# Weights issued sooner, token scores and token values later in the step, memory transposes of 64 columns

## The chip, the cores and the metric

The kernel runs on one core of one Trainium2 chip. The metric is the device time of one execution in microseconds (us). Three runs of the kernel before took 1035.26, 1035.57 and 1038.22 us; the median is 1035.57 us.

The core has five engines with an instruction queue each: TensorE (PE, with its weight loads shown apart as PEld), VectorE (DVE), ScalarE (ACT), GpSimd (POOL) and SyncE (SP). SP issues most DMAs; ACT and POOL can issue some too. An instruction at the head of a queue that has to wait for another engine holds up all that stands behind it on its own engine.

## The reference

A pre-normed attention with a memory that is carried from segment to segment, and a feed-forward layer behind it. The sequence of 2048 tokens (width 640) is cut into 64 segments of 32 tokens. Each segment attends to itself and to 8 memory rows, and the memory rows of its output are the memory of the next segment. So the 64 segments follow one another:

```python
mem = mem0
for s in range(n_seg):                       # 64
    h = concat([mem, xs], axis=1)            # 8 + 32 rows of 640
    q, k, v = h @ Wq, h @ Wk, h @ Wv         # 32 heads of 128
    p = softmax(mask(q @ k.T * scale))
    o = (p @ v) @ Wo
    mem = o[:, :M]                           # the next segment's memory
    outs.append(o[:, M:])
h = x + attention(layernorm(x))
out = h + relu(layernorm(h) @ w1 + b1) ** 2 @ w2 + b2
```

## The kernel before

Four segments are a block `b` of 128 tokens, and a segment is a step `s = 4*b + sp`. A program for each engine is written out by hand: `tc.manual_schedule(engines=None)` (L104) means that each engine runs its instructions in the order in which the Python code issues them. So where a line stands in `step` decides what it waits behind.

A segment's 40 rows are split in two. 32 of them (8 memory rows and the first 24 tokens) go through the step itself: they fill 32 columns of the array, and four such matmuls stand side by side in the 128 columns (`proj`, L194 to L204; the profile writes 128*32). The last 8 tokens of each segment, the tails, are projected for four segments at once, ahead of time: `tail_units` (L257) makes units of four matmuls each, and lists of them (`fill`) are run where PE would otherwise wait. A tail's queries and keys are put in place by `tails_in` (L312, POOL), its values are written to DRAM (`tail_out`, L272) and read back by `tails_v_in` (L321). The output product of four segments' tails is another list of units (`wo_tail_units`, L285).

One step (`step`, L368), in the order of PE's queue:

- four projections, two of queries and two of keys (L204, twenty matmuls each), each evacuated by ACT (L220, L222, L393) and turned over by DVE (L225, L396); POOL spreads the memory's queries (`spread`, L357);
- the memory rows' scores, first half (`scores(0)`, L404 and L409), then DVE's maximum (L415) and ACT's exponential (L418);
- two groups of the value projection (L473), half of the tokens' scores (`token_scores(0)`, L480 and L484), the other three groups (L490);
- DVE divides and turns over the memory's probabilities (`soft2(0)`, L424 to L428);
- two groups of the second value projection, `scores(1)`, `token_scores(1)`;
- `token_values` of the segment before (L343, L348), `values(0)` of this one (L437, L442), the last three groups of values (L512);
- DVE takes the tokens' maximum and subtracts it (L520, L522);
- the output product (`wo_rounds`, L236) in three parts, with `values(1)` after the first and one fill unit after the second (L526 to L532);
- ACT's exponential of the tokens' scores (L535), DVE's sum and reciprocal (L537, L539), POOL's products (L541, L544);
- `wo_out` (L239): ACT copies half of the product (L243), DVE adds the other half (L244); that is the segment's output `o`. Meanwhile PE runs 4 or 6 fill units (L556);
- `mem_to_hT` (L304): twenty small matmuls turn the memory rows of `o` into the columns that the next step's projections need, and DVE copies them into `hT` (L310); then `tails_in`, and the rest of the fill;
- DVE turns over the tokens' probabilities (L562, L568), for the token values of the next step.

The PSUM tiles are few: three for projections (`mm`), one (`chn`) shared by `scores`, `wo_rounds` and `mem_to_hT`, one (`po`) for the values.

Ahead of the loop, the weights are loaded by SP in the order in which they stand in the code: x of block 0, the memory, the tail rows, Wv (five DMAs of 1 MB), the next tail rows, Wq, x of block 1, Wk, and Wo in four DMAs (L134 to L145 and L709 to L717). `start` (L662) projects the first step's 40 rows and the first tails as the weights come in; with its v, `step` is called as "ready" and leaves out its own projections. Behind the loop, the feed-forward layer runs over four tiles of 512 tokens (L787 to L846).

Of the kernel before, what the change touches and what calls it, by code (L numbers as in the profile page):

```python
# [16 lines left out]
def kernel(  # L17
# [16 lines left out]
    nc = tc.nc  # L34
# [43 lines left out]
    ident = const.tile([128, 128], BF16)  # L78
    make_identity(nc, ident[:])
# [22 lines left out]
    oTts = [const.tile([128, H, 32], BF16, name="oTt%d" % k) for k in range(2)]  # L102

# [25 lines left out]
    o_ring = [const.tile([128, DH], BF16, name="o%d" % k) for k in range(5)]  # L129
    for o in o_ring:  # L130
        nc.gpsimd.memset(o[64:128], 0.0)
    o0 = o_ring[-1]
    nc.vector.memset(o0[0:64], 0.0)
    load_x(0)  # L134
    for ch in range(2):
        nc.sync.dma_start(out=o0[32 * ch:32 * ch + M, :].rearrange("m (c f) -> m c f", f=64),
                            in_=A_mem0[0].rearrange("m (c t f) -> t m c f", t=2, f=64)[ch])
    load_tail_rows(0)
    load_w(wv, A_Wv)
    def load_wo():  # L140
        wov = A_Wo.rearrange("h e d -> e h d")
        for n in range(2):
            for j in range(2):
                hs = slice(16 * j + n, 16 * j + n + 15, 2)
                nc.sync.dma_start(out=wo[:, hs, :], in_=wov[:, hs, :])  # L145
# [28 lines left out]
    def ln_transpose(b):  # L174
# [6 lines left out]
        def out():  # L181
            if isinstance(b, tuple):
                hTt = s2.tile([128, DC, 4, TL, 4], BF16, tag="hTt", name="hTt")
                nc.scalar.copy(out=hTt[:].rearrange("p c b k s -> p (c b) s k"),
                               in_=pt[:, 0:640].rearrange("p (a s k) -> p a s k", s=4, k=TL))
                hTts[b[1]] = hTt
                return
# [59 lines left out]
    fill, late, mid, win = [], [], [], []  # L247
# [24 lines left out]
    def tail_out(b, which, n, ps):  # L272
        row = parked.pop(0) if which == "v" and 0 < b and parked else rowtile()[:]
        evac_row(which, row, ps)
        if which == "v":
            eng = nc.sync if b else nc.scalar
            eng.dma_start(out=vt_d[b, 2 * n:2 * n + 2].rearrange("j r f -> r j f"),
                          in_=row.rearrange("r (j f) -> r j f", j=2))
# [25 lines left out]
    def mem_to_hT(o, hT4, sp):  # L304
        pm = chn.tile([128, 512], F32, tag="ch", name="pm")
        for c in range(DC):
            for q in range(4):
                nc.tensor.matmul(pm[32 * q:32 * q + 32, c * M:(c + 1) * M], lhsT=o[:, (2 * c + q % 2) * 32:(2 * c + q % 2 + 1) * 32],  # L308
                                 rhs=ident[:, q // 2 * 32:q // 2 * 32 + M], start=True, stop=True)
        nc.vector.tensor_copy(out=hT4[:, :, sp, 0:M], in_=pm[:, 0:DC * M].rearrange("p (c m) -> p c m", m=M))  # L310

    def tails_in(b, sp):  # L312
        q, k = [tails[b][w][:].rearrange("p h (k s) -> p h s k", s=4)[:, :, sp, :] for w in "qk"]
        nc.gpsimd.tensor_copy(out=qT[:, :, SEG:NK], in_=q)
        nc.gpsimd.tensor_copy(out=kT[:, :, SEG:2 * SEG].rearrange("p h (j k) -> p h j k", k=TL),  # L315
                              in_=k.unsqueeze(2).to_broadcast([128, H, 4, TL]))

    vt4s = {}
# [17 lines left out]
    def token_values(s, v, vt4, po):  # L336
# [3 lines left out]
        for i in range(HG):  # L340
            for g in range(G):
                r = slice(32 * g, 32 * g + 32)
                nc.tensor.matmul(po[:, g, i * 32:(i + 1) * 32], lhsT=v[r, i * E:(i + 1) * E], rhs=pTk[r, i, :],  # L343
                                 start=(i == 0), stop=False, skip_group_check=True)
# [23 lines left out]
    def step(b, sp, v=None):  # L368
# [62 lines left out]
        def values(n, pT, po):  # L431
            c0 = 256 + n * 4 * M
            for j in range(4):
                i = n * 4 + j
                for g in range(G):
                    r = slice(32 * g, 32 * g + 32)
                    nc.tensor.matmul(po[:, g, c0 + j * M:c0 + (j + 1) * M], lhsT=v[r, i * E:(i + 1) * E],  # L437
                                     rhs=pT[r, j * M:(j + 1) * M], start=(s == 0 and i == 0), stop=False,
# [11 lines left out]
        if not last and not ready:  # L450
            spread(0)
        if not last:
# [7 lines left out]

        if ready:
            tails_v_in(0, nc.gpsimd)
# [11 lines left out]
        sk = mmtile()  # L474
        skv = sk[:, 0:HG * NK].rearrange("p (i k) -> p i k", k=NK)

        def token_scores(n):
            if n == 0:
                for g in range(G):
                    nc.tensor.matmul(skv[32 * g:32 * g + 32, :, M:NK], lhsT=ident[:, 0:32], rhs=mask[:],  # L480
                                     start=True, stop=False, skip_group_check=True)
            for j in range(4):
                for g in range(G):
# [395 lines left out]
```

## Time and profile before

| what | value |
|---|---|
| three runs | 1035.26, 1035.57, 1038.22 us |
| profiled execution, its own time | 1037.09 us |
| its span in the profile | 1034.9 us, 2.2 us less than its time |
| PE busy | 973.5 us, 94% of the span, 26960 matmuls |
| DVE busy | 616.4 us, 60% |
| ACT busy | 533.5 us, 52% |
| POOL busy | 311.4 us, 30% |
| loads and stores by DMA | 51.58 MB |
| stretch up to 71.3 us | start and first step |
| stretch from 71.3 to 885.4 us | steps 1 to 62 |
| rest | last step and feed-forward layer |

A line of the timeline reads: start in us from the span's start, duration in us, engine, line, operation, output <- inputs, shape and count, and in brackets how long the engine had been idle ahead of it and what ended the wait. "issue" is time in which an engine waited for nothing that the profile shows. In a matmul's shape, 128*32 is the part of the array that it uses (rows by columns), and 128x512 is its moving operand. DVE, ACT and POOL busy shares are averages; what counts for a step is the chain from one step's `hT` to the next.

### The profile page before, as it was taken

What the parts mean: (1) busy time and instruction counts of PE and PEld (TensorE: products, weight loads), DVE (VectorE), ACT (ScalarE), POOL (GpSimd) and SP (SyncE); (2) the same over time, 40 slices, a digit from 0 to 9 for tenths busy, and PEclk for the clock granted to TensorE, in tenths of its full rate; (3) what the DMA queues carried; (4) which work ended last, traced back from release to release, by engine and by line L of the source; (5) the groups of instructions that cost most, each with busy time, mean ns of one, the idle gap of its engine ahead of it and who ended that gap; (6) DMA issues with size and microseconds to landing.
All of it is one profiled execution on the core that took longest, in us unless ns stands there. A gap on an engine that the chain in (4) does not pass through costs nothing.

```text
span 1034.9 us, 58969 instructions
## 1 busy us (share of the span) xinstructions
PE 973.5 (94%) x26960; PEld 572.4 (55%) x26960; DVE 616.4 (60%) x1740; ACT 533.5 (52%) x1225; POOL 311.4 (30%) x805
## 2 busy tenths in 40 slices
PE   4779899999999999999999999999999999999998
PEld 2335455555655555565555565565556565555565
DVE  2245666766666666666666666666665576565432
ACT  2425555555555555555555555555555555534431
POOL 1033333333333332232323232323233333343210
PEclk9989999999999999999999999999999999999999
DMA  8960100000100000000000000000000110512200
GB/s 321 405 203 26 23 7 28 9 22 8 28 14 22 14 25 23 14 21 14 27 14 21 15 27 14 22 15 27 15 21 9 46 34 6 195 55 71 77 26 26
DMA packets 39112, 51.58 MB, mean 50 GB/s; under 512 B 6160, under 2 KB 34960, under 8 KB 36944
## 3 DMA queue, kind: packets, MB, share of 16 engines
q1 hardware_dynamic: 38000, 47.30, 13.8%
q8 instruction: 210, 3.44, 1.4%
q14 instruction: 38, 0.31, 0.1%
q0 software_dynamic: 320, 0.26, 0.1%
q10 hardware_dynamic: 544, 0.26, 0.1%
HBM read 38.37 MB, written 9.44 MB: 46 GB/s over the span
## 4 chain that ended last, share of the span: by engine, by line
PE 87%; DMA 5%; issue 3%; DVE 2%; ACT 1%; POOL 0%; SPq 0%; DVEq 0%; ACTq 0%; POOLq 0%
PE ps L204 48%; PE pw L236 15%; PE y L830 6%; PE ps L798 5%; PE ps L236 3%; DMA xt<-in_A_x_dram 3%; PE po L437 2%; PE po L343 2%; PE sm L409 2%; DMA wq<-in_B_w_dram 1%; PE ps L484 1%; PE pm L308 1%; PE ps L480 1%; DMA vt<-vt_d 1%; DVE o L244 1%
## 5 line engine op out<-in xcount | busy, mean ns | idle before, releaser
L204 PEld LDWEIGHTS <-hT 128*32 128x32 bf16 x7680 | 193.4, 96 | 178.4 <-issue 14.5
L236 PE MATMUL pw<-wo,oT 128*32 128x320 bf16 x4224 | 184.9, 300 | 5.4 <-issue 4.3
L204 PE MATMUL ps<-wv,hT 128*32 128x512 bf16 x2520 | 171.2, 380 | 3.3 <-issue 2.6
L204 PE MATMUL ps<-wq,hT 128*32 128x512 bf16 x2520 | 158.2, 379 | 4.9 <-DVE hT L310 4.9
L204 PE MATMUL ps<-wk,hT 128*32 128x512 bf16 x2520 | 158.1, 379 | 0.1
L236 PEld LDWEIGHTS <-oT 128*32 128x32 bf16 x4224 | 104.7, 96 | 59.5 <-issue 11.8
L220 ACT ACTIVATE row<-ps 128x512 bf16<-128x512 f32 x156 | 93.3, 599 | 74.1 <-PE ps L204 72.8
L541 POOL TENSOR_TENSOR pkt<-ek,rk 128x64 bf16<-128x64 bf16 x64 | 18.8, 294 | 366.1 <-DVE rk L539 366.1
L225 DVE STREAM_TRANSPOSE qT<-row 128x512 bf16<-128x512 bf16 x128 | 90.2, 705 | 53.0 <-ACT row L220 53.0
L222 ACT CAST row<-ps 128x512 bf16<-128x512 f32 x115 | 67.9, 591 | 38.6 <-PE ps L204 38.5
L315 POOL COPY kT<-kTt 128x1024 bf16<-128x1024 bf16 x64 | 71.7, 1120 | 12.6 <-DVE kTt L225 12.6
L362 POOL COPY qz<-qT 128x96 bf16<-128x96 bf16 x126 | 33.4, 265 | 139.0 <-DVE qT L225 135.3
L204 PEld LDWEIGHTS <-hTt 128*32 128x32 bf16 x1920 | 53.1, 99 | 36.6 <-issue 6.0
L243 ACT COPY otmp<-pw 64x320 f32<-64x320 f32 x66 | 27.9, 422 | 81.0 <-PE pw L236 81.0
L353 ACT CAST oT<-po 128x512 bf16<-128x512 f32 x128 | 68.7, 589 | 1.6
L244 DVE TENSOR_TENSOR o<-pw,otmp 64x320 bf16<-64x320 f32 x66 | 31.8, 482 | 61.0 <-ACT otmp L243 61.0
L513 ACT CAST v<-ps 128x512 bf16<-128x512 f32 x63 | 36.9, 585 | 60.6 <-PE ps L204 60.6
L225 DVE STREAM_TRANSPOSE kT<-row 128x512 bf16<-128x512 bf16 x65 | 46.0, 709 | 29.7 <-ACT row L222 29.7
L537 DVE TENSOR_REDUCE zk<-ek 128x8 f32<-128x320 bf16 x64 | 31.1, 486 | 53.6 <-ACT ek L535 53.6
L830 PE MATMUL y<-wq,wk 128*128 128x320 bf16 x416 | 60.9, 299 | 0.0
L393 ACT CAST row<-ps 128x256 bf16<-128x256 f32 x126 | 40.7, 375 | 30.1 <-PE ps L204 30.1
L491 ACT CAST v<-ps 128x512 bf16<-128x512 f32 x63 | 36.9, 585 | 30.5 <-PE ps L204 30.5
(114 smaller groups left out, 1635.2 us busy)
## 6 DMA issues: line engine op xcount, KB each, us to landing
wv<-in_A_Wv_dram SPq DMA_DIRECT2D x5, 1024.0 KB
wq<-in_A_Wq_dram SPq DMA_DIRECT2D x5, 1024.0 KB
wk<-in_A_Wk_dram SPq DMA_DIRECT2D x5, 1024.0 KB
wo<-in_A_Wo_dram SPq DMA_DIRECT2D x4, 1280.0 KB
vt<-vt_d SPq DMA_DIRECT2D x60, 64.0 KB
xt<-in_A_x_dram SPq DMA_DIRECT2D x20, 160.0 KB
vt_d<-row SPq DMA_DIRECT2D x22, 128.0 KB
wq<-in_B_w_dram SPq DMA_DIRECT2D x1, 2080.0 KB
```

The costliest lines, as they stand in the source:

```text
L204: nc.tensor.matmul(ps[32 * k:32 * k + 32, :], lhsT=lhs(c), rhs=wr[:, c, n, k], start=(c == 0), stop=(c == DC - 1))
L220: nc.scalar.mul(out=row, in_=ps, mul=scale)
L222: nc.scalar.copy(out=row, in_=ps)
L225: nc.vector.transpose(out=dst[:, n * 16:(n + 1) * 16, 0:32], in_=row.rearrange("p (h e) -> p h e", e=32))
L236: nc.tensor.matmul(pw[32 * j:32 * j + 32, 0:DH], lhsT=lhs(p), rhs=wov2[:, head(p), ch], start=(h == 0), stop=(h == 15))
L244: nc.vector.tensor_tensor(out=o[0:64], in0=pw[0:64, 0:DH], in1=tmp[0:64], op=ALU.add)
L315: nc.gpsimd.tensor_copy(out=kT[:, :, SEG:2 * SEG].rearrange("p h (j k) -> p h j k", k=TL), in_=k.unsqueeze(2).to_broadcast([128, H, 4, TL]))
L353: nc.scalar.copy(out=oTg[:, n, :, :, M:NK], in_=po[:, :, n * 128:(n + 1) * 128].rearrange("p g (j q) -> p g j q", q=32))
L393: nc.scalar.copy(out=row[:, u * 256:(u + 1) * 256], in_=ps[:, u * 256:(u + 1) * 256])
L491: nc.scalar.copy(out=v[:, 0:512], in_=ps0[:])
L798: nc.tensor.matmul(ps[:], lhsT=w1[:, c, fc * 128:(fc + 1) * 128], rhs=hnT[:, c, :], start=(c == 0), stop=(c == DC - 1))
L830: nc.tensor.matmul(y[:, hh, 0:DH], lhsT=f1T[:, fc, k * 128:(k + 1) * 128], rhs=w2[:, fc, cs], start=(fc == 0), stop=False, skip_group_chec ...
```

## The change

- Loads: the memory is loaded through ACT's queue, so that SP goes on to the tail rows and Wv without waiting; x of block 1 goes behind Wk and Wo, and its norm and transposes go from `start` into steps 1 and 2; Wo comes in six pieces, the heads that the product needs first ahead of the others; the stores of the tails' values of blocks 1 to 4 are put off to step 1.
- Start: the tails' queries and keys are put in place in halves; `tails_v_in(0)` and ten units of block 4's tail values go between the query and key projections, and ten units of block 1's tail keys behind the key projection, instead of into the first step.
- Step: `token_scores` is one piece and goes behind `values(1)`, between the two halves of the output product; `token_values` goes behind the whole output product, in the place of two of the fill units that stood there; the fill unit within the product is gone. The tokens' exponential goes behind ACT's L243, and the chain behind it goes into the next step in two parts: `soft_a` (L537 to L544) behind the first query projection, `soft_b` (L562 to L568) behind the second. `tails_in` goes ahead of the fill.
- `mem_to_hT`: ten matmuls of 64 columns in place of twenty of 32.

```diff
     def load_wo():
         wov = A_Wo.rearrange("h e d -> e h d")
-        for n in range(2):
-            for j in range(2):
-                hs = slice(16 * j + n, 16 * j + n + 15, 2)
-                nc.sync.dma_start(out=wo[:, hs, :], in_=wov[:, hs, :])
+        for h0, k in ((0, 8), (16, 8), (1, 4), (17, 4), (9, 4), (25, 4)):
+            hs = slice(h0, h0 + 2 * k - 1, 2)
+            nc.sync.dma_start(out=wo[:, hs, :], in_=wov[:, hs, :])
...
     def mem_to_hT(o, hT4, sp):
         pm = chn.tile([128, 512], F32, tag="ch", name="pm")
         for c in range(DC):
-            for q in range(4):
-                nc.tensor.matmul(pm[32 * q:32 * q + 32, c * M:(c + 1) * M], lhsT=o[:, (2 * c + q % 2) * 32:(2 * c + q % 2 + 1) * 32],
-                                 rhs=ident[:, q // 2 * 32:q // 2 * 32 + M], start=True, stop=True)
+            for ch in range(2):
+                nc.tensor.matmul(pm[64 * ch:64 * ch + 64, c * M:(c + 1) * M], lhsT=o[:, c * 64:(c + 1) * 64],
+                                 rhs=ident[:, 32 * ch:32 * ch + M], start=True, stop=True)
...
         project("q", wq, qT, 0)
         if not last and not ready:
             spread(0)
+        run(soft, 1)
...
         elif not ready:
             spread(1)
-
-        if ready:
-            tails_v_in(0, nc.gpsimd)
+        run(soft, 1)
...
-        token_scores(0)
...
-            proj(wv, "half", lhs, 1, ps1, 0, 2)
+            proj(wv, "half", lhs, 1, ps1, 0, 3)
         if not last:
             scores(1)
-        token_scores(1)
-        if not last:
             soft1(1)
...
-        if s:
-            token_values(s - 1, prev["v"], prev["vt4"], po)
         if not last:
             values(0, pT0, po)
             values_out(0, po)
         if not ready:
-            proj(wv, "half", lhs, 1, ps1, 2, DC)
+            proj(wv, "half", lhs, 1, ps1, 3, DC)
...
-        wo_rounds(main, pw, 0, 6)
+        wo_rounds(main, pw, 0, 8)
         if not last:
             values(1, pT1, po)
             values_out(1, po)
-        wo_rounds(main, pw, 6, 8)
-        run(fill, 1)
+        sk = mmtile()
+        skv = sk[:, 0:HG * NK].rearrange("p (i k) -> p i k", k=NK)
+        token_scores(skv)
+        mxk = s1.tile([128, HG], F32, tag="mxk", name="mxk")
+        nc.vector.tensor_reduce(out=mxk[:], in_=skv, op=ALU.max, axis=AX.X)
...
         wo_rounds(main, pw, 8, 16)
...
+        o = wo_out(pw)
         ek = s1.tile([128, HG, NK], BF16, tag="ek", name="ek")
-        nc.scalar.activation(out=ek[:], in_=tk[:], func=ACT.Exp, scale=1.0)
...
+        nc.scalar.activation(out=ek[:], in_=tk, func=ACT.Exp, scale=1.0)
         if s:
+            token_values(s - 1, prev["v"], prev["vt4"], po, last)
             token_out(s - 1, po)
...
-            run(fill, 4 if outs else 6)
+            run(fill, 2 if outs else 4)
             mem_to_hT(o, hT4s[(s + 1) // 4], (s + 1) % 4)
...
+        def soft_a():
+            zk = s1.tile([128, HG], F32, tag="zk", name="zk")
+            nc.vector.tensor_reduce(out=zk[:], in_=ek[:], op=ALU.add, axis=AX.X)
...
+            soft.append(lambda: soft_b(pkt, pk))
+
+        def soft_b(pkt, pk):
+            pTt = s1.tile([128, 2, 32], BF16, tag="pTt", name="pTt")
+            nc.vector.transpose(out=pTt[:], in_=pkt[:].rearrange("p (u j) k -> p u (j k)", u=2))
...
+            pTk = s1.tile([128, HG, 32], BF16, tag="pTk", name="pTk")
+            nc.vector.transpose(out=pTk[:], in_=pk[:])
+            back.append((pTk, pTx))
+
+        soft.append(soft_a)
...
         stream("q", wq, qT)
         for n in range(2):
             spread(n)
-        ln_transpose(1)()
-        units += tail_units(4, "v") + tail_units(1, "q")
+        tails_v_in(0, nc.gpsimd)
+        units += tail_units(4, "v")
+        run(units, 2 * DC)
+        units += tail_units(1, "q")
         stream("k", wk, kT)
+        units += tail_units(1, "k")
+        run(units, 2 * DC)
         run(late, 100)
...
-    load_x(1)
     load_w(wk, A_Wk)
     load_wo()
+    load_x(1)
```

## The prediction, made before the changed kernel ran

> **What bounds the kernel now.** I read the page, then the windows, then the timelines of the start and of one step. Page: the second slice line is PE's, then the queue that brings instructions, then the chain that ended last by engine.
>
> ```profile
> PE   4779899999999999999999999999999999999998
> ...
> q8 instruction: 210, 3.44, 1.4%
> ...
> PE 87%; DMA 5%; issue 3%; DVE 2%; ACT 1%; POOL 0%; SPq 0%; DVEq 0%; ACTq 0%; POOLq 0%
> ```
>
> PE sets the pace but for the first 70 us, so a step lasts as long as PE's work in it plus PE's waits. In the start the loads set it: in the windows (columns: PE, PEld, DVE, ACT, POOL, granted clock, DMA share, GB/s) the DMA engines are full until 60 us and PE's clock falls.
>
> ```profile
> 40.00:60.00 20.00, 14.06 (x272) 6.71 (x268) 5.80 (x13) 6.00 (x13) 4.00 (x6) 0.77 1.05 375
> 60.00:80.00 20.00, 16.20 (x443) 8.69 (x444) 10.09 (x31) 6.87 (x17) 4.29 (x12) 0.91 0.40 116
> ```
>
> The start's timeline: x of block 1 lands only at 35.46 and PE's key projection stands behind it (38.47); then PE waits 5.53 us for the tails' keys; step 1 begins at 71.28.
>
> ```profile
> 35.46 0.89 DVE L152 BATCH_NORM_STATS2 lnst<-xt 128x6 f32<-128x320 bf16 x2 [12.23 <-DMA xt<-in_A_x_dram]
> ...
> 54.62 0.40 PE L409 MATMUL sm<-kT,qz 128*32 128x64 bf16 x16 [5.53 <-POOL kT L315]
> ...
> 71.28 1.26 PE L204 MATMUL ps<-wq,hT 128*32 128x512 bf16 x20 [0.34 <-DVE hT L310]
> ```
>
> The step from 398.20 (first query projection) to 411.91 is the model for the loop:
>
> ```profile
> 402.30 0.71 DVE L225 STREAM_TRANSPOSE qT<-row 128x512 bf16<-128x512 bf16 x1 [0.38 <-ACT row L220]
> ...
> 402.94 0.22 DVE L415 TENSOR_REDUCE mx<-sm 128x1 f32<-128x64 f32 x1
> ...
> 404.28 0.25 DVE L428 STREAM_TRANSPOSE pTm<-pmem 128x64 bf16<-128x64 bf16 x1
> ...
> 405.04 0.29 PE L437 MATMUL po<-pTm,v 32*128 32x8 bf16 x15
> ...
> 406.31 0.09 PEld L437 LDWEIGHTS <-v 32*128 32x128 bf16 x1 [1.07 <-issue]
> ...
> 411.14 0.28 PE L308 MATMUL pm<-ident,o 128*32 128x8 bf16 x20
> ```
>
> DVE runs the last query transpose, then the maximum of `scores(0)`, and its probabilities are ready at 404.53; PE takes them at 405.04. So this chain has 0.45 us to spare, no more. The 1.07 us of "issue" is the other finding: PE stops with all its operands ready. The instruction queue's 210 packets of 16 KB are 257 instructions each for PE's 53920, and four such stops (379, 392, 405, 419 us) lie 768 PE instructions apart, three packets. After such a stop PE goes on 2.5 to 3.6 us after it passed the border one packet back, 3.05 taken as the middle. The Trainium skill ("Runtime: NRT & Kernel Launch", Instruction fetch mechanics) says that blocks of 256 instructions are fetched while the last one runs, mostly hidden; by the rule the stops would be nothing, and here they are not.
>
> Counted from one `scores(0)` to the next, 35 steps with ten fill units last 13.04 us on average (shortest 12.56), 14 steps with a whole output-tail product 13.45, six with five units 12.97, five with none 13.0. In the 49 full ones 0.3 to 0.4 us is such stops.
>
> **The step, part by part** (us from the start of the first query projection; hops of 0.05 between engines as the timeline has them).
>
> Work that PE keeps is conserved: projections 4 x 1.08, `scores` 2 x 0.14, values' projections 2 x 1.08, `values` 0.26 + 0.23, token scores 0.34, token values 0.28, product 64 matmuls 2.16, ten units 2.16, memory transposes 0.13: 12.3. What changes are the waits.
>
> `soft_b` puts L562 and L568 on DVE between the last query transpose and the maximum of `scores(0)`. These two take 0.48 (398.50 to 398.98 in the timeline). POOL's products for them come behind the reciprocal: DVE is free at 2.6, sum 0.5, reciprocal 0.2, POOL 0.3 + 0.6: ready at 4.3, ahead of DVE's 4.74, so no wait there. The maximum goes from 4.74 to 5.22, and everything behind it on DVE with it: L396 to 6.17 and the probabilities from 6.33 to 6.81, ready for PE at 6.86. PE's cover between `scores(0)` and `values(0)` was 0.43 + 0.21 + 0.65 + 0.43 + 0.14 + 0.23 + 0.28; the token scores (0.21 + 0.23) and values (0.28) leave, one group of values (0.22) comes: PE arrives at 4.32 + 0.14 + 1.08 + 0.65 + 0.14 = 6.33. So PE waits 0.53 in front of `values(0)`. Queued behind it are the values' projection and the product; ACT and DVE, waiting for them, are late next.
>
> Token scores stand between `values(1)` and the second half of the product, which needs ACT's L213: 0.61 from the last `values(1)` matmul in the timeline, against 0.11 + 0.34 of cover: 0.15 wait. The first half of the product must wait for DVE's L211: 0 to 0.1, take 0.05. Behind the product, `o` needs 1.30 (409.84 to 411.14), which six units (1.29) hid exactly; four units and token values are 0.86 + 0.28 = 1.14: wait 0.15. Token values also bring a second change of the array's tiling, which fits into this wait. Sum of waits 0.9, from 0.65 (all small ones gone) to 1.1. In their favour, today's wait of 0.12 for ACT's v in front of `values(1)` goes.
>
> Memory transposes: twenty matmuls take 0.13, 6.5 ns each, four side by side, so 26 ns for one place. Ten with two side by side: 0.13 again. But they are in another tiling than their neighbours: where the product is followed by 128-column transposes (L179) it takes 1.19 instead of 1.09. One such change hides in the wait for `o`, the other costs 0.1 (from -0.07, if ten take half of twenty's time, to 0.2). The Trainium skill ("TensorEngine Tiling (Array Packing)", Key Properties) says that a change of tiling mode drains the array, which speaks against this edit; it gives no price. Its cover for DVE's `hT` is now 1.29 of fill instead of 0.65, and 0.65 was enough.
>
> Stops for instructions: a step has 780 instead of 800. Densest run of 256 today: 24 matmuls of projection, `scores(1)`, token scores, values: 2.5 us; in the new order `values(1)`, token scores, half product, token values: 2.1 to 2.3, but the run around `values(0)` is stretched by its wait to 2.9. Sliding the border over the step with 3.05 us per 256, I get 0.55 today (the trace: 0.4) and 0.2 then.
>
> Full step: 12.3 + 0.9 + 0.1 + 0.2 = 13.5 against 13.04: +0.44, bounds -0.1 to +0.8. 49 of them: **+21.6** (-5 to +39). Steps without fill or with five units gain, since token values now cover 0.28 of their 1.3 wait and the rest of units come after: 12.75 against 12.97 and 12.6 against 13.0: 6 x 0.2 + 5 x 0.4 = **-3**.
>
> **The start.** SP now issues Wv at about 1.75 instead of 4.76 (the memory's 1.62 and the wait ahead of it leave; ACT issues them with nothing waiting there until 6.5). The packets run without a hole from 6.3 to 46 (Wk) and 61 us (Wo, 0.36 MB/us), so all comes 3.0 sooner, and x of block 1 (0.16 MB) another 0.4: Wk's last packet at 42.8, Wo's at 57.4. A load is usable some 1.6 behind its last packet (Wk: 46.2, used at 48.03). The keys are then done at 45.3 instead of 49.1, and DVE's seven remaining transposes put the first maximum at 51.1 instead of 55.07; block 0's values are there, where PE waited for them until 62.85. But now the product waits for Wo's last piece, 59.0, where before it began at 66.67 with Wo there: product 0.55, `o` 1.30, `hT` 0.63: step 1 at 61.5. After such idling the clock is at half for about 3.4 us (as 52.4 to 59.3 now), of which I charge 1.3: 62.8, **-8.5** (-11 to -5, the latter if the issue of Wk waits for ACT's stores and leaves a hole). Block 1's transposes go into step 2: **+0.4**. x of block 1 lands at 59.5, ahead of need. Last step: the moved chain hides behind `end_output`'s 64 matmuls: 0, at worst +1.
>
> **Sum.** 1037.1 (profiled) + 21.6 - 3 - 8.5 + 0.4 = 1047.6; the median lies 1.5 under the profiled execution: **1046**. Own range 1038 to 1058.
>
> **Rivals.**
> - *The loop loses less than the start gains.* The point is (8.5 + 3 - 0.4) / 49 = 0.23 us a step. For it: 0.4 us of stops might all be absorbed by the new waits, and the small waits may vanish: 12.3 + 0.65 = 12.95, -0.1 each, 1037.1 - 5 - 11.1 - 1.5 = 1019.5; the middle between that and break-even is 1027. Against it: the 0.48 on DVE and the 0.72 of cover taken from PE are read off the queue's order. Chance 0.20.
> - *Break even:* loss of 0.17 to 0.3 a step, 1035. Chance 0.07.
> - *The start doesn't gain:* Wk waits for a hole in the loads and the clock stays low; the loop loses as forecast: 1054. Chance 0.10, slower too.
> - *Forecast:* 0.63.
>
> So slower 0.73, within 0.3% (3 us, about what these runs can tell from nothing) 0.07, faster 0.20. Range 1024 to 1058: a tenth is left out on either side.
>
> **What would show it.** PE idle of about half a us in front of L437 of `values(0)`, ended by DVE's transpose, in nearly every step; the two transposes of `soft_b` directly ahead of the maximum; full steps of 13.5; fewer "issue" stops; L308 with ten matmuls in about the time of twenty; step 1 at about 63 us with the product waiting for Wo. Wrong if PE doesn't wait there, or if step 1 starts after 68 us.

## The result, and the profile after

The changed kernel takes 1060.94 us (median of 4 runs, 1059.37 to 1061.96), the kernel before, on the same chip and beside it, 1036.18 (1035.26 to 1038.22): a ratio of 1.0234, 95% interval 1.0215 to 1.0253. It is slower, as forecast, but by 24.8 us and not by 10, and it lies above the range. The profiled execution took 1060.08 us, span 1058.3.

From the page of the changed kernel, PE's slice line, the instruction queue and the chain that ended last by engine:

```profile
PE   5789899999999999999999999999999999999998
...
q8 instruction: 205, 3.36, 1.4%
...
PE 69%; DVE 17%; ACT 4%; DMA 4%; issue 2%; SPq 2%; POOL 0%; DVEq 0%; ACTq 0%; POOLq 0%
```

PE is still busy in every slice behind the start, so a step still lasts as long as its work and its waits. But in the chain DVE has gone from 2% to 17%: the chain now runs through DVE's transposes ahead of `values(0)` (L227, L406, L576 and L438 among its lines). The instruction queue has 205 packets instead of 210 for the ten matmuls fewer per step (and as many weight loads).

The spans differ by 23.4 us. Taken from the start of each step's first query projection: step 1 starts at 64.41 us instead of 71.28 (-6.9); from there to the start of the last step is 844.1 us instead of 814.2 (+29.9); from there to the end 149.8 instead of 149.5 (+0.3). Counted from one `scores(0)` to the next as in the prediction:

| steps | before, us | after, us | sum of the difference, us | forecast, us |
|---|---|---|---|---|
| 35 with ten fill units | 13.04 (shortest 12.56) | 13.70 (shortest 13.49) | +23.2 | |
| 14 with an output-tail product | 13.45 | 14.10 | +9.2 | the 49 full ones together: +21.6 |
| 6 with five units | 12.97 | 12.82 | -0.9 | the 11 together: -3 |
| 5 with none | 13.00 | 12.87 | -0.7 | |

A step of the changed kernel, from its timeline (start, duration, engine, line, output<-inputs, in brackets the idle time and what ended it; what the prediction calls L562, L568, L437 and L308 is now L570, L576, L447 and L316):

```profile
409.28 0.20 DVE L570 STREAM_TRANSPOSE pTt<-pkt 128x64 bf16<-128x64 bf16 x1
409.41 0.40 DVE L576 STREAM_TRANSPOSE pTk<-pk 128x256 bf16<-128x256 bf16 x1
...
409.73 0.18 DVE L425 TENSOR_REDUCE mx<-sm 128x1 f32<-128x64 f32 x1
...
410.69 0.29 PE L419 MATMUL sm<-kT,qz 128*32 128x64 bf16 x16
...
410.94 0.25 DVE L438 STREAM_TRANSPOSE pTm<-pmem 128x64 bf16<-128x64 bf16 x1
...
411.24 0.26 PE L447 MATMUL po<-pTm,v 32*128 32x8 bf16 x16 [0.26 <-DVE pTm L438]
...
413.53 0.27 ACT L215 CAST oT<-po 128x128 bf16<-128x128 f32 x1 [0.81 <-PE po L452]
...
413.85 1.27 PE L238 MATMUL pw<-wo,oT 128*32 128x320 bf16 x32
...
415.06 0.37 PE L353 MATMUL po<-pTk,v 32*128 32x32 bf16 x32
...
415.44 1.05 PE L206 MATMUL ps<-wk,hTt 128*32 128x512 bf16 x16
...
415.63 0.48 DVE L246 TENSOR_TENSOR o<-pw,otmp 64x320 bf16<-64x320 f32 x1 [0.61 <-ACT otmp L245]
...
416.42 0.32 PE L316 MATMUL pm<-ident,o 128*64 128x8 bf16 x10
416.67 1.48 PE L206 MATMUL ps<-wk,hTt 128*32 128x512 bf16 x24
```

The two transposes of `soft_b` stand directly ahead of the maximum, and PE waits in front of `values(0)` for the last link of that chain. The 0.26 in brackets is idle time behind a modelled end; from the start of the last matmul of `scores(1)` (410.79, the last of the sixteen in the row at 410.69) the gap is 0.45, 0.44 more than from one such matmul to the next. Not all of it is DVE's: in e1 below, where nothing is waited for at this place, the same gap is still 0.12, because the tiling of the array changes here. So what DVE's chain adds is 0.33. At the memory transposes there is no such bracket: `o` is ready at 416.11, and PE comes to them only at 416.42. They start 0.25 ahead of the units behind them, where twenty took 0.13 before.

PE's waits between 130 and 860 us (matmul, what it waited for: us in total, times, longest), first before, then after:

```profile
PE po L437 <- issue: 6.0, 13, 1.0
PE pw L236 <- issue: 3.8, 10, 0.6
PE pm L308 <- DVE o L244: 3.7, 8, 1.1
```

```profile
PE po L447 <- DVE pTm L438: 14.5, 53, 0.3
PE po L358 <- issue: 2.3, 5, 0.6
PE pm L316 <- DVE o L246: 1.0, 2, 0.7
```

The stops for instructions have mostly gone, and 53 waits for DVE have come. All gaps of PE over 0.23 us that stand at the border of 256 of PE's instructions, between 85 and 860 us, number 47 with 29.5 us before and 25 with 11.0 us after; below they are called the stops.

In the start, the windows (columns as before) and PE's timeline of the changed kernel:

```profile
40.00:60.00 20.00, 13.22 (x312) 7.09 (x305) 6.92 (x18) 6.16 (x14) 2.75 (x6) 0.91 1.06 352
60.00:80.00 20.00, 16.84 (x456) 9.08 (x452) 10.65 (x33) 8.70 (x21) 6.42 (x17) 1.00 0.32 93
```

```profile
47.84 0.76 PE L206 MATMUL pa<-wk,hT 128*32 128x512 bf16 x8 [3.52 <-DMA wk<-in_A_Wk_dram]
...
62.03 0.72 PE L238 MATMUL pw<-wo,oT 128*32 128x320 bf16 x14 [1.44 <-DMA wo<-in_A_Wo_dram]
...
64.41 1.26 PE L206 MATMUL ps<-wq,hT 128*32 128x512 bf16 x20 [0.30 <-DVE hT L318]
```

Step 1 now starts behind a product that waits for Wo, as forecast. But Wk's last piece is used at 47.84, hardly sooner than the 48.03 of before, and Wo's last piece comes at 62.03. The clock was granted in full from 60 us on.

### The profile page after: what moved, and what is told of

It reads as the page before. It is cut to its first block, busy times and chain, and to the rows that moved or that the text cites. A ratio compares the mean times of both kernels' runs of the same rounds, so it can differ in the third digit from the quotient of the medians.

```text
span 1058.3 us, 57841 instructions
## 1 busy us (share of the span) xinstructions
PE 1000.5 (95%) x26311; PEld 582.1 (55%) x26320; DVE 597.1 (56%) x1740; ACT 537.2 (51%) x1229; POOL 310.5 (29%) x807
## 3 DMA queue, kind: packets, MB, share of 16 engines
q8 instruction: 205, 3.36, 1.4%
## 4 chain that ended last, share of the span: by engine, by line
PE 69%; DVE 17%; ACT 4%; DMA 4%; issue 2%; SPq 2%; POOL 0%; DVEq 0%; ACTq 0%; POOLq 0%
PE ps L206 30%; PE pw L238 15%; PE y L854 5%; PE ps L822 5%; DVE qT L227 4%; DVE kT L406 4%; PE ps L238 3%; ACT row L222 3%; PE po L447 3%; DVE pTk L576 2%; PE po L353 2%; DVE pTm L438 1%; PE pm L316 1%; DVE pmem L436 1%; PE ps L491 1%
## 5 line engine op out<-in xcount | busy, mean ns | idle before, releaser
L206 PEld LDWEIGHTS <-hT 128*32 128x32 bf16 x7680 | 200.6, 97 | 188.4 <-issue 14.0
L238 PE MATMUL pw<-wo,oT 128*32 128x320 bf16 x4224 | 170.4, 300 | 4.4 <-issue 1.5
L206 PE MATMUL ps<-wv,hT 128*32 128x512 bf16 x2520 | 158.6, 380 | 0.0
L365 POOL COPY oTt<-oT 128x256 bf16<-128x256 bf16 x64 | 26.8, 419 | 440.9 <-ACT oT L363 342.8
L227 DVE STREAM_TRANSPOSE qT<-row 128x512 bf16<-128x512 bf16 x128 | 90.7, 709 | 80.4 <-ACT row L222 79.5
L238 PEld LDWEIGHTS <-oT 128*32 128x32 bf16 x4224 | 101.8, 96 | 56.1 <-DVE oT L213 23.2
L530 DVE TENSOR_REDUCE mxk<-ps 128x8 f32<-128x320 f32 x64 | 31.5, 492 | 94.6 <-PE ps L491 94.6
L325 POOL COPY kT<-kTt 128x1024 bf16<-128x1024 bf16 (+1 forms) x65 | 71.0, 1092 | 12.0 <-DVE kTt L227 12.0
L206 PEld LDWEIGHTS <-hTt 128*32 128x32 bf16 x1920 | 46.0, 97 | 39.6 <-issue 5.5
L428 ACT ACTIVATE em<-sm,mx 128x64 bf16<-128x64 f32 x126 | 39.6, 314 | 54.4 <-DVE mx L425 54.4
L830 ACT ACTIVATE wv<-ps,b1f 128x512 bf16<-128x512 f32 (+1 forms) x56 | 37.6, 672 | 28.5 <-PE ps L822 27.7
L227 DVE STREAM_TRANSPOSE kT<-row 128x512 bf16<-128x512 bf16 x65 | 43.0, 662 | 12.7 <-ACT row L224 12.7
```

Of the source, the lines that this page charges most:

```text
L206: nc.tensor.matmul(ps[32 * k:32 * k + 32, :], lhsT=lhs(c), rhs=wr[:, c, n, k], start=(c == 0), stop=(c == DC - 1))
L227: nc.vector.transpose(out=dst[:, n * 16:(n + 1) * 16, 0:32], in_=row.rearrange("p (h e) -> p h e", e=32))
L238: nc.tensor.matmul(pw[32 * j:32 * j + 32, 0:DH], lhsT=lhs(p), rhs=wov2[:, head(p), ch], start=(h == 0), stop=(h == 15))
L325: nc.gpsimd.tensor_copy(out=kT[:, h0:h1, SEG:2 * SEG].rearrange("p h (j k) -> p h j k", k=TL), in_=k.unsqueeze(2).to_broadcast([128, h1 - ...
L428: nc.scalar.activation(out=em[:], in_=sms[n][:, 0:2 * SEG], func=ACT.Exp, bias=mx[:, 0:1], scale=1.0, accum_out=zm[:])
```

## The experiments

Every kernel here computes the whole reference. "Shortest" and "mean" are the steps with ten units, from `scores(0)` to `scores(0)`. The kernel before, run beside them on the same chip, had medians of 1036.78 to 1038.36 us. The theory (A in the expectations; C in those of e7 and e9 is what it says of the stops alone): the loop loses at three places that can be undone one by one, namely `soft_b` on DVE, the 64-column transposes and the late token values, each by what PE then waits or pays; what the waits hid of the stops comes back. The rivals stand in each expectation.

| kernel | median, us (range) | ratio to before, 95% | shortest, mean, us | step 1 at, us | stops, us |
|---|---|---|---|---|---|
| before | 1036.18 | | 12.56, 13.04 | 71.28 | 29.5 |
| after | 1060.94 | 1.0234 (1.0215 to 1.0253) | 13.49, 13.70 | 64.41 | 11.0 |
| e1 | 1045.98 (1044.72 to 1046.61) | 1.0087 (1.0063 to 1.011) | 13.30, 13.41 | 63.81 | 6.7 |
| e2 | 1054.92 (1053.56 to 1055.23) | 1.0172 (1.0149 to 1.0195) | 13.25, 13.54 | 64.70 | 19.7 |
| e3 | 1046.10 (1044.84 to 1047.96) | 1.0085 (1.0058 to 1.0113) | 13.00, 13.38 | 64.10 | 21.7 |
| e4 | 1033.12 (1031.09 to 1034.69) | 0.9960 (0.9947 to 0.9973) | 12.56, 13.06 | 63.83 | 28.8 |
| e5 | 1048.64 (1047.99 to 1051.28) | 1.0114 (1.0085 to 1.0143) | 12.80, 13.21 | 71.04 | 24.4 |
| e6 | 1041.04 (1037.31 to 1042.08) | 1.0021 (1.0005 to 1.0037) | 13.06, 13.29 | 65.03 | 14.2 |
| e7 | 1019.24 (1017.42 to 1019.88) | 0.9828 (0.9798 to 0.9858) | 12.79, 12.82 | 63.84 | none |
| e8 | 1042.95 (1041.02 to 1045.83) | 1.0045 (1.0027 to 1.0063) | 12.56, 13.21 | 69.59 | 35.1 |
| e9 | 1016.61 (1015.46 to 1018.58) | 0.9798 (0.9777 to 0.982) | 12.79, 12.83 | 63.70 | 6.5 |
| e10 | 1103.27 (1100.03 to 1105.74) | 1.0631 (1.0605 to 1.0657) | 13.34, 14.27 | 64.09 | 26.3 |
| e11 | 1061.51 (1060.74 to 1062.6) | 1.0241 (1.0214 to 1.0269) | 13.49, 13.68 | 64.00 | 9.7 |
| e12 | 1015.31 (1014.65 to 1018.58) | 0.9799 (0.9772 to 0.9826) | 12.79, 12.87 | 65.72 | 6.5 |

### e1: the rest of the token softmax later on DVE

```diff
         elif not ready:
             spread(1)
-        run(soft, 1)
...
         if not last:
             pT1 = soft2(1)
+        run(soft, 1)
```

> The changed kernel (1060.9 us) with the two transposes of soft_b moved on DVE from in front of the maximum of scores(0) to behind the turned-over probabilities of the second half, where DVE idles 1.47 us. Theory A (the wait of about 0.44 us in front of values(0) is made by these two transposes): the maximum comes 0.48 us sooner, PE's wait for L438 goes to under 0.1 us, the shortest full step falls from 13.49 to about 13.2 us, and the time to 1041 to 1047 us. Theory B (PE is held by the delivery of its instructions, and the wait only hides such stops): the wait goes, but as many stops come, time above 1055 us.

The row for `values(0)` is gone from PE's waits; what is left between 130 and 860 us is led by

```profile
PE po L358 <- issue: 1.7, 5, 0.4
PE pm L316 <- DVE o L246: 1.0, 2, 0.7
```

and the kernel is 15 us faster than the changed one. So the wait is `soft_b`'s, shown by taking it away. The shortest step falls by 0.19, not by the 0.44 of idling, for two reasons: 0.11 of the 0.44 is the change of tiling, which stays, and from the last values' projection to the product 0.64 is now seen instead of 0.49, since DVE's eviction of the first values, which the product needs, is late next (0.33 - 0.15 = 0.18). The mean falls by 0.29, since there are fewer stops too (6.7 us instead of 11.0).

### e2, e5, e6: the memory transposes

e2 is the changed kernel with the old transposes, e5 the kernel before with the new ones, e6 has the edits of e1 and e2. The edit, in e5's direction:

```diff
-            for q in range(4):
-                nc.tensor.matmul(pm[32 * q:32 * q + 32, c * M:(c + 1) * M], lhsT=o[:, (2 * c + q % 2) * 32:(2 * c + q % 2 + 1) * 32],
-                                 rhs=ident[:, q // 2 * 32:q // 2 * 32 + M], start=True, stop=True)
+            for ch in range(2):
+                nc.tensor.matmul(pm[64 * ch:64 * ch + 64, c * M:(c + 1) * M], lhsT=o[:, c * 64:(c + 1) * 64],
+                                 rhs=ident[:, 32 * ch:32 * ch + M], start=True, stop=True)
```

> The changed kernel (1060.9 us) with the memory transposes back at twenty matmuls of 32 columns; nothing else. Theory A (each change of the array's tiling costs some 0.11 us, and the 64-column matmuls add two per step that are on PE's path): 0.24 us less in each of 62 steps, 1044 to 1049 us. Rival (ten matmuls cost about what twenty cost, the changes hide in the wait for o): 1058 to 1064 us.

> The kernel before (1036 us) with the 64-column memory transposes alone. Theory A (two tiling changes of 0.12 us on PE's path in each of 62 steps, part of it given back because stops for instructions get shorter when a step is slower): shortest full step 12.56 + 0.24 = 12.80 us, time 1042 to 1048 us. Rival (the edit is free): 1033 to 1039 us.

> The changed kernel (1060.9 us) with both edits of the first two runs: soft_b behind the second half's probabilities, and memory transposes of 32 columns. Theory A (the two add, less some stops for instructions that come back): shortest full step 13.49 - 0.2 - 0.24 = 13.05 us, time 1036 to 1042 us. Rival (the stops eat the second one): above 1043 us.

The price is the same both ways: the shortest step falls by 0.24 in e2 and rises by 0.24 in e5. It lies on both sides of the transposes, as the starts of neighbouring groups show. In e2 (old transposes) sixteen matmuls of fill are followed by the transposes after 0.87 us, where in the changed kernel they are followed after 0.98 (415.44 to 416.42); and from the transposes to the next fill the changed kernel has 0.25 where twenty took 0.13. So ten matmuls of 64 columns are worth what twenty of 32 are, and each of the two changes of tiling costs 0.11 to 0.12, none of it hidden. e6, with the edits of e1 and e2 together, came out as expected: a shortest step of 13.06 and 1041.04 us.

e2's time was a miss: 6 us faster instead of at least 11.9. From its timeline:

```profile
414.88 1.05 PE L206 MATMUL ps<-wk,hTt 128*32 128x512 bf16 x16
415.75 0.22 PE L316 MATMUL pm<-ident,o 128*32 128x8 bf16 x10
416.43 0.23 PE L316 MATMUL pm<-ident,o 128*32 128x8 bf16 x10 [0.46 <-issue]
416.50 1.48 PE L206 MATMUL ps<-wk,hTt 128*32 128x512 bf16 x24
```

In the middle of the twenty transposes PE stops with everything it needs there: 20 instructions more in the step and 0.24 us less of time bring the stops back, 19.7 us of them instead of 11.0. The 62 x 0.24 = 14.9 saved, less these 8.7, is the 6 measured. The same holds for e5, with stops of 24.4 instead of 29.5; its 1048.64 is a little above the expected 1042 to 1048.

### e3 and e9: the token values

e3 puts the token values of the changed kernel back in front of `values(0)`; e9 takes the new start alone (e4, below) and moves only the token values behind the output product.

```diff
         po = pop.tile([128, G, 512], F32, tag="po", name="po")
-        if s:
-            token_values(s - 1, prev["v"], prev["vt4"], po)
         if not last:
             values(0, pT0, po)
...
         o = wo_out(pw)
         if s:
+            token_values(s - 1, prev["v"], prev["vt4"], po, last)
             token_out(s - 1, po)
...
-            run(fill, 4 if outs else 6)
+            run(fill, 2 if outs else 4)
```

That is e9; e3 is the same in the other direction, on the changed kernel.

> The changed kernel (1060.9 us) with token values back in front of values(0) and 6 (4) fill units in front of the memory transposes again. Theory A (behind the output product they cost two tiling changes of 0.11 us, and in front of values(0) they would cover most of the wait there, sharing its tiling): the tail of a step from the second half of the product to the next step falls from 4.1 to about 3.6 us, the wait in front of values(0) under 0.15 us, time 1033 to 1043 us, with more stops for instructions than the changed kernel. Theory B (delivery of instructions): the gain is eaten by stops, above 1052 us.

> The changed kernel's start with the old step (1033.1 us), and of the step's edits token values behind the output product alone (in the place of two fill units, as in the change); token scores, the chain behind them and the memory transposes are the old ones. Theory C (two tiling changes more, 0.2 us in a step, but the dense runs of instructions are torn apart, so that the stops at borders of 256 go from 29 us to under 9 us, and steps without fill gain 0.3 us): shortest full step 12.75 to 12.85 us, time 1016 to 1025 us. Rival (this move is what made the change slow): 1040 us and more.

One and the same move costs 15 us in one order and gains 16.5 in the other (1033.12 to 1016.61). In the changed kernel the token values in front of `values(0)` are 0.28 of cover for DVE's late chain: with them back, all but 0.05 of the wait there is gone, the two changes of tiling around them at the end of the step go too (0.21), and the shortest step falls by the sum, from 13.49 to 13.00; the stops, 21.7 instead of 11.0, take back a part, so that e3 is 3 us above what was expected. e9 came out as expected. In the old order there is no wait to cover. There the move lengthens the shortest step by 0.23, to 12.79, and the rows say where: the second product half takes 1.20 instead of 1.09 and the token values 0.38 instead of 0.28, again a change of tiling on either side. But it takes the stops from 28.8 to 6.5 us, and the steps with five units fall from 12.81 in e4 to 12.51, since the token values now hide a part of their wait for `o` (PE's waits for `o` between 130 and 860 us: 3.7 us in e4, 1.4 in e9).

### e4: the start alone

The loads and the start of the changed kernel, with the step and the transposes of before. One part of it:

```diff
-    load_x(1)
     load_w(wk, A_Wk)
     load_wo()
+    load_x(1)
```

> The kernel before (1036 us) with the changed kernel's start and loads alone; the step is the old one. Theory A: the start's gain (6.9 us to step 1 in the profile of the changed kernel) stays, 1027 to 1031 us. Rival (the start's gain needs the new order of the step, or is given back in the first steps): 1034 to 1038 us.

The truth lay between the two: 1033.12, 4.0 us faster. Step 1 begins 7.45 us sooner, but its first two projections run at half clock (granted clock 0.56; 1.93 us from one to the next where 1.08 is usual), so 1.7 us are given back. The edit is worth about 4 to 5 us on the old step, and 6.9 in the changed kernel's profile, whose step 1 found the full clock.

### e7: is it the density of PE's instructions?

e4 with the token values moved forward, in between the projections, where they break up nothing else:

```diff
             project("k", wk, kT, 0)
+            po = pop.tile([128, G, 512], F32, tag="po", name="po")
+            if s:
+                token_values(s - 1, prev["v"], prev["vt4"], po)
         project("q", wq, qT, 1)
```

> The changed kernel's start with the old step (1033.1 us), and token values moved from in front of values(0) to between the first key and the second query projection of the same step, where PE's instructions are least dense. Theory C (PE can't go on sooner than some 3 us after the last border of 256 instructions; stops there cost 29 us in the kernel before): shortest full step longer by two tiling changes, 12.56 + 0.25 = 12.8 us, but the stops at these borders fall from 29 us to under 8 us: 1018 to 1027 us. Rival (the stops have another cause, or come elsewhere): 1033 us plus 15 us for the changes of tiling, 1040 us and more.

PE's waits between 130 and 860 us, all rows:

```profile
PE pm L316 <- DVE o L246: 3.7, 8, 1.1
PE ps L206 <- DVE hT L318: 3.5, 10, 0.4
PE ps L206 <- ACT v L502: 0.7, 1, 0.7
PE ps L491 <- ACT row L403: 0.2, 1, 0.2
```

As theory C had it, no row says "issue" any more. The number of instructions is that of before (210 packets); only forty small matmuls have moved from a place with many small ones to one with long ones. The shortest step is 0.23 longer and the mean 0.22 shorter. So the stops depend on how many instructions PE takes in a short time.

The records of the instruction queue show what PE stops for. In the kernel before, each of the 39 stops of over 0.3 us between 85 and 860 us ended 1.2 to 1.6 us after a packet of this queue had been moved; at the 146 borders without such a stop the last packet lay 1.2 to 5.4 us back, 2.8 in the middle. A packet takes 1.07 us (median), and no two of the 210 start less than 3.36 us apart. And the 256 instructions ahead of a stop took 2.5 us in the middle, those ahead of the other borders 4.5 (21 of those 146 took under 3 us, so the time of the last 256 alone does not decide it): where PE runs through a packet's worth of instructions faster than the next packet comes, it stops.

### e8 and e10: the late token softmax

e8 is the kernel before with only the two `soft_b` transposes moved ahead of the maximum. e10 is e4 with the token scores behind `values(1)` and the softmax of them at the end of the same step, so that nothing stands in front of the maximum of the next.

```diff
             project("k", wk, kT, 0)
         elif not ready:
             spread(1)
+        run(soft, 1)
...
-        pTt = s1.tile([128, 2, 32], BF16, tag="pTt", name="pTt")
-        nc.vector.transpose(out=pTt[:], in_=pkt[:].rearrange("p (u j) k -> p u (j k)", u=2))
+        def soft_b(pkt=pkt, pk=pk):
+            pTt = s1.tile([128, 2, 32], BF16, tag="pTt", name="pTt")
+            nc.vector.transpose(out=pTt[:], in_=pkt[:].rearrange("p (u j) k -> p u (j k)", u=2))
...
+        soft.append(soft_b)
```

That is e8; parts of e10:

```diff
-        token_scores(0)
...
-        token_scores(1)
...
-        wo_rounds(main, pw, 0, 6)
+        wo_rounds(main, pw, 0, 8)
         if not last:
             values(1, pT1, po)
             values_out(1, po)
...
+        token_scores(skv)
...
         wo_rounds(main, pw, 8, 16)
+        o = wo_out(pw)
         ek = s1.tile([128, HG, NK], BF16, tag="ek", name="ek")
...
+        zk = s1.tile([128, HG], F32, tag="zk", name="zk")
+        nc.vector.tensor_reduce(out=zk[:], in_=ek[:], op=ALU.add, axis=AX.X)
...
         run(mid, 2)
         run(fill, 100)
```

> The kernel before (1036 us) with soft_b alone moved on DVE in front of the maximum of scores(0), as the change has it; token scores and values stay. Theory A (the chain to values(0) has 0.45 us to spare there and the move takes 0.48): a wait of under 0.1 us in front of values(0), 1034 to 1041 us. Rival (the move costs its 0.48 us wherever it stands): 1055 us and more.

> The changed kernel's start with the old step (1033.1 us), and of the step's edits the token scores behind values(1) alone (with the exponential behind ACT's first half of o, the fill unit within the product gone, and the rest of their softmax at the end of the step, where it stood); token values and memory transposes are the old ones. Theory A (0.15 us of wait for L215 in each step, and the stops for instructions at about 20 to 29 us as before): shortest full step 12.7 to 12.8 us, 1034 to 1043 us. Rival (the late scores alone make the wait in front of values(0)): shortest full step above 13.0 us, 1050 us and more.

e8: 4.6 us slower by the ratio (1042.95, 2 us above the expected range), 5.6 of more stops, the shortest step unchanged and no row of waiting for the probabilities. So 0.48 us more on DVE cost nothing by themselves as long as the token scores and values stand between `scores(0)` and `values(0)`. The wait of the changed kernel needs both: the transposes on DVE and the cover taken from PE.

e10 was missed: 1103 us instead of at most 1043. The number and the shortest step, 13.34, lie where the rival put them, but not for its reason: no row of PE's waits names `values(0)`. The timeline around the end of a step with an output tail:

```profile
450.10 1.10 POOL L325 COPY kT<-kTt 128x1024 bf16<-128x1024 bf16 x1
...
451.17 0.29 POOL L559 TENSOR_TENSOR pkt<-ek,rk 128x64 bf16<-128x64 bf16 x1
...
451.49 0.24 DVE L567 STREAM_TRANSPOSE pTt<-pkt 128x64 bf16<-128x64 bf16 x1 [1.62 <-POOL pkt L559]
...
452.43 0.44 DVE L246 TENSOR_TENSOR o<-ps,otmp 64x320 bf16<-64x320 f32 x1
...
452.93 1.26 PE L206 MATMUL ps<-wq,hT 128*32 128x512 bf16 x20 [0.78 <-DVE o L246]
```

POOL's product for the softmax stands behind its copies of the tails' keys; DVE waits 1.62 us for it; behind that wait stand the tail's `o` and the query transposes, and PE waits for `o`. In the next `scores(0)`, 22.8 us of waits for DVE's transposes and 16.8 for POOL's copies are found between 130 and 860 us, and 6.9 of waits for `o`; that is about two thirds of the 70 us by which e10 lies above e4, and the rest was not traced. Of the places tried for the chain behind the late scores, the end of the step holds up DVE, and the one ahead of the maximum holds up `values(0)`; in e1's place for its transposes, behind the probabilities of the second half, no wait for them was left.

### e11 and e12: what holds Wk back in the start

In the changed kernel POOL issues the loads of block 0's token values ahead of the keys, at 38.67 us, where before they ran at 58 to 62. The rates of the DMA engines together from 40 to 50 us, in slices of 0.25 us, before and after:

```profile
GB/s 426 459 459 361 393 426 426 492 426 328 459 393 459 361 328 426 459 459 393 360 459 426 313 319 406 383 390 362 347 369 358 379 353 369 353 369 358 364 364 369
```

```profile
GB/s 393 295 426 426 459 426 328 393 459 492 360 282 303 388 282 287 315 244 302 239 288 304 263 288 265 276 266 241 369 364 348 374 343 384 348 374 364 353 379 348
```

The full busy share is there in both, but from 43.5 to 47 us the changed kernel moves 0.24 to 0.32 MB/us where before it was 0.31 to 0.46. e11 (the changed kernel) and e12 (e9) issue these loads on SP, behind Wk and ahead of Wo:

```diff
         stream("v", wv, None)
+        tails_v_in(0, nc.sync)
+        load_wo()
+        load_x(1)
...
-        tails_v_in(0, nc.gpsimd)
...
     load_w(wk, A_Wk)
-    load_wo()
-    load_x(1)
```

> The changed kernel, but the four loads of block 0's token values (vt) are issued by SP behind Wk and ahead of Wo, not by POOL at 38.67 us. Theory A (these loads took the DMA engines from Wk's last pieces: from 42 to 47 us all queues together moved only 0.26 to 0.32 MB/us in place of 0.42, and Wk's last piece was used at 47.84 us and not at the 44.4 forecast): the fall in the rate goes, Wk's last piece is used at 45.0 to 46.0, Wo's second half is there about 1 to 1.5 us sooner, step 1 starts at 62.7 to 63.5 instead of 64.41; median 1058.5 to 1060.5. Rival (the rate fell because Wo's smaller packets run beside Wk's last ones): Wk's last piece still at 47 or later, step 1 at 64.4 plus or minus 0.4, 1060.5 to 1062.

> The same move of the four loads on the version with the new start and the token values behind the output product (1016.61 us, step 1 at 63.70). Theory A: step 1 at 62.0 to 62.8, median 1015.0 to 1016.0, with the loop's steps as they were (full steps 12.8). Rival: step 1 at 63.7, 1016 to 1018. If Wk comes sooner but step 1 does not start sooner, Wo's last piece alone sets the start and what the loads of the token values cost is hidden behind it.

PE's start in e11:

```profile
46.04 0.67 PE L206 MATMUL pa<-wk,hT 128*32 128x512 bf16 x8 [2.45 <-DMA wk<-in_A_Wk_dram]
...
61.61 0.72 PE L238 MATMUL pw<-wo,oT 128*32 128x320 bf16 x14 [1.48 <-DMA wo<-in_A_Wo_dram]
...
64.00 2.32 PE L206 MATMUL ps<-wq,hT 128*32 128x512 bf16 x20 [0.29 <-DVE hT L318]
```

Wk's last piece is used 1.8 us sooner, as theory A had it, but Wo's comes only 0.4 sooner and step 1 starts only 0.4 sooner, and then at half clock (granted 0.50 from 64 to 66 us): 1061.51, no gain. In e12 step 1 starts even later, at 65.72, for Wo's last piece comes at 62.75 and the granted clock is 0.50 from there on, and the time is that of e9 within the ranges. The rate falls in e11 too (0.21 to 0.29 MB/us from 43.5 to 47), so POOL's queue is not its cause.

The kernel before shows the same fall at another place. There the four loads run later, and from 59.5 to 60 us, beside Wo alone, the engines together move 0.28 MB/us, where from 49 to 55, without them, they move 0.36. A packet of Wo (1280 bytes) takes 60 ns in the mean without these loads beside it and 72 to 92 ns with them, in all three kernels. Wo's packets beside Wk's last ones, the rival in e11, don't do it: before, from 45 to 47 us, both run together, and Wo's packets take 58 ns. So the fall goes with these loads, at three dates and in two queues; by what mechanism stays open, and a kernel without them was not run. For the start it is shown that Wo's last piece sets it, and that Wk's date no longer matters.

e9, and e12 with it, is the fastest version: 2.0% under the kernel before (0.9777 to 0.982), 4.2% under the changed one (1016.61 / 1060.94). e7 (1.7% under) and e4 (0.4% under) beat the kernel before too.

## Why the prediction missed

**The direction and the chief wait were right.** PE idles in front of `values(0)` until DVE's last transpose, 0.44 where 0.53 was forecast, in nearly every step (a change of tiling of 0.11 hides in it, which the forecast did not have); `soft_b` directly ahead of the maximum; its two conditions, the DVE time and the lost cover, both needed (e1, e3, e8). The small waits for the evictions of the values are there in their sizes too: that of the first product half for DVE's, forecast 0.05, with 0.06 (0.49 from `values(0)` to the product for eight matmuls of 0.43), that of the second half for ACT's, forecast 0.15, with 0.13.

**The step that failed is "Work that PE keeps is conserved", 12.3 us, with 0.1 for the changes of tiling.** The 12.3 adds up each piece at its smallest row, and the prediction then charged a single 0.1, because "One such change hides in the wait for `o`" and the token values' change "fits into this wait". That wait does not exist. Piece by piece in the step at 408.80, from start to start:

| piece | before, us | forecast, us | after, us |
|---|---|---|---|
| projections, `scores` | 4.32 + 0.28 | 4.32 + 0.28 | 4.32 + 0.28 |
| values' projections, with the wait in front of the product | 2.17 | 2.16 + 0.05 | 1.73 + 0.49 |
| `values` | 0.22 + 0.22 | 0.26 + 0.23 | 0.22 + 0.23 |
| token scores | 0.21 + 0.23 | 0.34 | 0.33 |
| product | 0.92 + 0.28 + 1.09 | 2.16 | 1.20 + 1.20 |
| token values | 0.28 | 0.28 | 0.38 |
| ten units | 0.22 + 1.29 + 0.65 | 2.16 | 0.98 + 1.30 |
| memory transposes | 0.13 | 0.13 + 0.10 | 0.25 |
| the other waits | | 0.53 + 0.15 + 0.15 | 0.44 + 0.13 |
| stops | 0.48 | 0.2 | 0.21 |
| sum | 13.0 | 13.5 | 13.7 |

(The stops are here the mean less the shortest step; before is the step at 398.20 without its stop.) The waits of the prediction are there but for one: 0.44 for the probabilities, and 0.13 between the token scores and the second product half, where ACT's L215 ends at 413.80 and the product starts at 413.85. The wait for `o` is not: PE comes to the memory transposes 0.3 late by its own work. What made it late are four changes of tiling which the old order had not, around the token values and around the memory transposes: 0.11 in the product, 0.10 in the token values, 0.12 in the units, 0.12 in the transposes, 0.45 in all where 0.1 was charged. e2 and e5 show the second pair by taking it away and adding it (0.24), e9 the first (0.23). Another 0.13 was there before already and was read away in the 12.3: the change within the first product half (0.92 for 24 matmuls, where 32 without one take 1.09). So the work was 0.45 too small and the waits 0.25 too large; the two errors partly cancel, and 0.2 is left. Over the 49 full steps the difference to before is +32.4 us instead of +21.6, and these 10.8 are most of the 12.5 by which the profiled execution lies above the forecast's sum (1060.08 against 1047.6); the median, at last, lies 0.9 above it and not 1.5 below.

The Trainium skill ("TensorEngine Tiling (Array Packing)", Key Properties) says that a change of tiling mode drains the array. The times of these runs fit that and give the price, 0.10 to 0.12 us; the prediction should have counted the changes in the new order as it counted the matmuls.

**The stops went as forecast**: 0.2 a step, and 11.0 us over 62 steps are 0.18. And e2, e3 and e7 show that they come and go with the density of instructions, as the prediction had it. The Trainium skill ("Runtime: NRT & Kernel Launch", Instruction fetch mechanics) has the fetch mostly hidden; here 29.5 of 1036 us were not.

**The start** gave 6.9 in the profile instead of 8.5. "All comes 3.0 sooner" failed: up to 42 us the engines had moved 1.0 MB more than before, but at 58 us only 0.57, with 0.26 MB of token values among it, which now run ahead of Wo's end and slow the other packets (e11 and e12). The lost lead of 0.44 MB and these 0.26 are 1.9 us at Wo's 0.36 MB/us. Wo's last piece came at 62.03 instead of 59.0; the rest of these 3.0 us was not traced. That 1.3 was charged for a half clock which the profile did not show hid half of the miss; e4 and e11, with step 1 at the same place, do show it. (The stretch that the prediction names for it, 52.4 to 59.3 us, lasts twice 3.4 us.)

**The steps without fill and with five units** fell by 0.13 and 0.15 instead of 0.4 and 0.2, 1.4 us more in all. The rivals in which the loop loses less or breaks even fell; "the start doesn't gain" fell too: 7 us is a gain, and the excess lies in the loop.

## What to carry to other kernels

Count the changes of array tiling in the new order of the matmuls and price each from a row where such a change stands, before giving any of it to a wait; a wait hides work only if it is still there with that work in place. A move is worth what its new neighbours make of it: the token values behind the product gained 16.5 us where nothing waited in front of `values(0)` and cost 15 where DVE's chain did. Where PE stops for instructions with all operands ready, spread the small matmuls among long ones, even at the price of a longer shortest step.

## What had not been expected of the hardware

Ten transposing matmuls of 64 columns, 8 wide, were no faster than twenty of 32 (from the first to the last start 0.15 us against 0.12). The stops were at the same instruction of each 256 in every kernel that had them, whatever line stood there, and one placement of forty small matmuls took 28.8 us of them to none. Packets of the instruction queue never started less than 3.36 us apart in the kernel before. Four loads of 64 KB brought the engines' rate from 0.36 to 0.42 MB/us down to 0.25 to 0.29, at full busy share, wherever they stood. The granted clock around step 1 differed between kernels that reached it at nearly the same time: a first projection of 1.08 us in the changed kernel at 64.41, and of 1.93 in e4 at 63.83.
